# A decode step of two attention and two gated layers: one more quarter of a key cache kept in PSUM, all other products in four banks

## The chip, the cores and the metric

The kernel runs on one core of a Trainium2 chip. The metric is the device time of one execution in microseconds. A difference is given against the kernel before, which computes the same.

## The reference

One token for each of two sequences goes through attention, a gated feed-forward layer, and both again with the same weights and the same caches. All data are fp32.

```python
# B=2, H=32 heads, Sk=8192 cached rows, Dh=128, D=576, Df=4608
def attention(x):                      # x: [B, 1, D], after layernorm
    q = (x @ wq) split into heads
    scores = einsum("bhqd,bhkd->bhqk", q, k_cache) * Dh ** -0.5
    o = einsum("bhqk,bhkd->bhqd", softmax(scores), v_cache)
    return o.reshape(B, 1, H * Dh) @ wo
def glu(x):
    return (gelu(x @ w_gate) * (x @ w_up)) @ w_down
x = x + attention(layernorm(x)); x = x + glu(layernorm(x))
x = x + attention(layernorm(x)); x = x + glu(layernorm(x))
```

A key or value cache of one head of one sequence has 8192 rows of 128 numbers, 4.19 MB. There are 64 of each, so one pass over both caches reads 537 MB, and two passes read them twice, except for what is kept on the chip in between.

## The kernel before

**Items.** Attention works through 64 heads (32 heads, 2 sequences) as 34 items, `ITEMS`: items 0 to 29 are pairs of heads, and the last four, 30 to 33 (`SINGLE[0]` to `SINGLE[3]`), are single heads. The first attention takes the items in rising order, the second in falling order, so that it begins with what the first had last. A pair's keys are 8 parts, a single head's 4 parts; a part is 128 x 2048 fp32, 1.05 MB.

**Space.** One SBUF tile, `space`, holds all that is loaded: six slots of four parts each, the sixth shared with a ring of four places. `Arena` decides at build time which place each load gets and which release it waits for. All loads go through one queue on SyncE, in the order in which `plan_first`, `plan_mlp` and `plan_second` list them. A load is issued when the place that it overwrites is free, and later loads stand behind it.

**Kept items.** At the end of the first attention the keys of items 32 and 33 and the values of items 31, 32 and 33 stay in SBUF (`KEYS_HELD`, `VALUES_HELD`) and are not read again. For kept keys the first attention writes its products elsewhere. The second attention reloads the keys of 31 and 30, first those of 31 into the ring, then those of 30 into the places of the keys of 33 as these are used up, and so on (`plan_second`, `one`).

**One item.** `query` spreads the item's query over the partitions with matmuls (into `qp`, two buffers). For each part, `multiply` forms the products on VectorE (L511), GpSimd adds their halves (L515), and VectorE sums the rest (`add_up`, L518). During the next item's parts the softmax of this item follows: `peak` (maximum, L532, and its transpose `mT`, L534), `highest` (L540, and `nb`, L542), `softmax` (ScalarE, `nbs` at L563 and the exponentials at L565), `total` (`tot`, L574, and its reciprocal, L577 or L582). `values` multiplies the weights with the value cache on TensorE into `acc` (L604). `gather` (L618, L620), `context` (`po`, L629) and `divide` (`oT`, L636 or L645) bring out the head's result, and `project` (L657) adds its part of the output into `xps`.

The order is written out by hand in the loop of `attention`: it is the program's order on every engine, and each engine works in that order. For part 2 of an item it is

```python
if k == 2:
    if p is not None:
        total(p)
    if a is not None:
        gather(a)
        if p < PAIRS:
            context(a)
    if v is not None and v >= 0:
        values(v)
    if a is not None and p >= PAIRS:
        context(a)
```

where `p` is the item before, `v` the item whose values are due, and `a` the one whose accumulator is complete. Where `p` is a single head, the context matmuls stand behind the value matmuls.

**PSUM.** There are eight banks of 128 x 512 fp32. Before, `acc` has two, `xps` one, `po` one, the queries `qp` two, and the other small products (`every4`, `mT`, `nb`, `tot`, with the tag `small`) two. Each is a tile of its own, and waits between engines follow the tiles.

Of the kernel before, what the change touches and what calls it, by code (L numbers as in the profile page):

```python
# [9 lines left out]
F32 = mybir.dt.float32  # L10
# [112 lines left out]
def decode_layers(ctx, tc, x_in, kc, vc, wq, wo, wg, wu, wd, out):  # L123
# [6 lines left out]
    psum1 = ctx.enter_context(tc.tile_pool(name="psum1", bufs=1, space=PSUM))  # L130
    psum2 = ctx.enter_context(tc.tile_pool(name="psum2", bufs=2, space=PSUM))
    ctx.enter_context(tc.manual_schedule())
# [201 lines left out]
    def plan_second():  # L334
# [3 lines left out]
        k63, v63, k62, v62 = ("k", 1, SINGLE[3]), ("v", 1, SINGLE[3]), ("k", 1, SINGLE[2]), ("v", 1, SINGLE[2])  # L338
        for k in range(4):
            one(("k", 1, SINGLE[1]), kc, SINGLE[1], k, None)  # L340
        for k in range(4):
            one(("k", 1, SINGLE[0]), kc, SINGLE[0], k, (k63, k))

        for kind, k in (("k", 0), ("v", 0), ("v", 1), ("k", 1), ("v", 2), ("v", 3), ("k", 2), ("k", 3)):
            if kind == "k":
                one(("k", 1, last), kc, last, k, (k62, k))
            else:
                one(("v", 1, SINGLE[0]), vc, SINGLE[0], k, (v63, k))
        for k in range(4):
            one(("k", 1, last), kc, last, 4 + k, (v62, k))  # L350
        half(("k", 1, last - 1), kc, last - 1, 0, 5)
# [77 lines left out]
    for s in range(2):  # L429
        nc.vector.memset(acc[:, s, :], 0.0)  # L430
    xps = psum1.tile([P, CW], F32, name="xps")
    nc.vector.memset(xps, 0.0)


    def norm(split=False):
# [5 lines left out]
        )  # L441
        every4 = psum2.tile([P, 4 * 6], F32, name="every4", tag="small")
        nc.tensor.matmul(every4, same, apart.rearrange("p c t -> p (c t)"), start=True, stop=True)
# [27 lines left out]
    def attention(layer):  # L471
# [14 lines left out]
        qb, S, prod, rs, mT, rinv, osb = {}, {}, {}, {}, {}, {}, {}  # L486
        po = psum1.tile([P, GH, 2], F32, name="po")

# [3 lines left out]
        def query(n):  # L492

            it = ITEMS[n]
            qb[n] = psum2.tile([P, DH], F32, name="qp")
            for i in range(it.heads):
# [7 lines left out]
        def multiply(n, k):  # L504

            if k == 0:
                S[n] = work.tile([P, SK * 2 // P], F32, name="S")
            u = t = ready[name("k", layer, n)][k]
            if layer == 0 and n in KEYS_HELD:
                u = ready["products"][k % 2]  # L510
# [6 lines left out]
        def add_up(n, k):  # L517
            nc.vector.tensor_reduce(  # L518
                out=S[n][:, k * JC:(k + 1) * JC], in_=prod.pop((n, k)), axis=AX.X, op=ALU.add
            )  # L520
            if layer == 0 and n in KEYS_HELD:
                if n == N - 1 and k >= 2:
                    done(("products", k - 2))
                return
            key = name("k", layer, n)
            done((key, k))
            if k == ITEMS[n].parts - 1:
                ready.pop(key)

        def peak(n):  # L530
            m = work.tile([P, 1], F32, name="m")
            nc.vector.reduce_max(m, S[n][:, :ITEMS[n].rows], axis=AX.X)  # L532
            mT[n] = psum2.tile([1, P], F32, name="mT", tag="small")
            nc.tensor.transpose(mT[n], m, ident)  # L534

        def highest(n):
# [3 lines left out]
            nc.vector.reduce_max(m1[:, :heads], mT.pop(n).rearrange("p (i q) -> p i q", i=heads), axis=AX.X)  # L540
            mT[n] = psum2.tile([P, 2], F32, name="nb", tag="small")
            nc.tensor.matmul(mT[n][:, :heads], ones[0:1, :], m1[:, :heads], start=True, stop=True)  # L542
# [28 lines left out]
        def total(n):  # L571
            it = ITEMS[n]
            tot = psum2.tile([P, 2], F32, name="tot", tag="small")
            nc.tensor.matmul(tot[:, :it.heads], ones, rs.pop(n), start=True, stop=True)  # L574
# [259 lines left out]
```

## Time and profile before

| | us |
|---|---|
| median of 3 runs | 2697.15 |
| lowest and highest run | 2696.98, 2701.9 |
| the profiled execution | 2700.58 |
| its span, first to last instruction | 2698.8 |

The profile is one execution. Its rows give starts in us from the span's start. "PE" is TensorE, "DVE" VectorE, "ACT" ScalarE, "POOL" GpSimd, "SP" SyncE, whose queue issues the loads. A row of the timeline has the start, the duration, the engine, the line of the kernel, what is written and read, the count, and in brackets the idle time of the engine just before with what ended it. A row of the windows has the busy time of each engine in that stretch, the granted TensorE clock, the DMA share and GB/s. Stages: the first attention lasts until about 1295, the first gated layer until about 1373, the second attention until about 2623.

### The profile page before, as it was taken

How to read it: one execution, taken by the hardware profiler on the slowest of the kernel's cores; microseconds unless marked ns; L12 is line 12 of the kernel's file. 1: busy time of each engine (PE TensorE's matmuls, PEld its weight loads, DVE VectorE, ACT ScalarE, POOL GpSimd, SP SyncE). 2: the span in 40 equal slices, each digit the busy share in tenths (PEclk: the TensorE clock that was granted, in tenths of full speed). 3: DMA queues.
4: the chain of work that ended last, by engine and by line, in shares of the span. 5: the costliest groups of instructions: out<-in, count | busy, mean ns of one | idle time of the engine just before them, and what ended most of it. 6: DMA issues, size and time to landing. Idle time of an engine off the chain costs nothing.

```text
span 2698.8 us, 17988 instructions
## 1 busy us (share of the span) xinstructions
PE 900.1 (33%) x7020; PEld 294.0 (11%) x7020; DVE 1872.1 (69%) x1688; ACT 90.0 (3%) x399; POOL 1210.8 (45%) x528
## 2 busy tenths in 40 slices
PE   1323331333233223334644332333233323322355
PEld 0100010001000000111211110001000100000022
DVE  4877787678777776776039887778767867777740
ACT  0000000000000000000000000000000000000000
POOL 2644454445445444544016554445444544544420
PEclk7656656665666566666766665665566566656677
DMA  9999999999999999999999999999999999999998
GB/s 420 435 434 434 434 434 433 433 432 434 435 433 432 435 432 430 433 428 422 403 378 421 429 427 436 435 430 434 434 434 431 434 434 432 434 433 436 432 421 378
DMA packets 33524, 1155.39 MB, mean 428 GB/s; under 512 B 3976, under 2 KB 4000, under 8 KB 5536
## 3 DMA queue, kind: packets, MB, share of 16 engines
q1 hardware_dynamic: 33400, 1154.24, 99.5%
q8 instruction: 55, 0.90, 0.1%
q14 instruction: 29, 0.24, 0.0%
q10 hardware_dynamic: 40, 0.01, 0.0%
HBM read 1154.23 MB, written 0.00 MB: 428 GB/s over the span
## 4 chain that ended last, share of the span: by engine, by line
DMA 82%; DVE 15%; PE 1%; issue 1%; POOL 1%; ACT 0%; SPq 0%; ACTq 0%; DVEq 0%; POOLq 0%
DMA space<-in_A_k_cache_dram 75%; DVE space L511 9%; DVE S L518 5%; DMA space<-in_B_w_up_dram 3%; DMA space<-in_A_wo_dram 2%; DMA space<-in_B_w_down_dram 2%; POOL space L515 1%; DMA space<-in_A_wq_dram 1%; PE acc L742 0%; DMA space<-in_B_w_gate_dram 0%; DMA x<-in_A_x_dram 0%; PE xps L791 0%; PE acc L604 0%; PE acc L478 0%; DVE osb L620 0%
## 5 line engine op out<-in xcount | busy, mean ns | idle before, releaser
L515 POOL TENSOR_TENSOR space<-space 128x1024 f32<-128x1024 f32 x512 | 1206.8, 2357 | 1245.2 <-DVE space L511 1230.4
L511 DVE TENSOR_TENSOR space<-space,qp 128x2048 f32<-128x2048 f32 x512 | 1166.0, 2278 | 591.7 <-DMA space<-in_A_k_cache_dram 567.9
L604 PE MATMUL acc<-space,prz 128*8 128x512 f32 x4096 | 591.3, 740 | 452.2 <-DMA space<-in_A_v_cache_dram 447.6
L518 DVE TENSOR_REDUCE S<-space 128x16 f32<-128x1024 f32 x512 | 618.9, 1209 | 3.4 <-POOL space L515 3.4
L534 PE MATMUL mT<-ident,m 128*1 128x128 f32 x68 | 24.8, 365 | 804.9 <-DVE m L532 804.9
L604 PEld LDWEIGHTS acc<-space,prz 128*8 128x8 f32 x4096 | 118.2, 104 | 868.4 <-DMA space<-in_A_v_cache_dram 452.1
L563 ACT ACTIVATE nbs<-nb 64x1 f32<-64x1 f32 (+1 forms) x128 | 21.2, 166 | 2333.7 <-PE nb L542 2333.0
L534 PEld LDWEIGHTS mT<-ident,m 128*1 128x1 f32 x68 | 5.4, 79 | 821.9 <-issue 786.5
L629 PE MATMUL po<-of,osb 128*32 128x2 f32 x512 | 40.9, 202 | 130.9 <-DVE osb L620 130.9
L542 PE MATMUL nb<-m,unit 1*128 1x2 f32 (+1 forms) x136 | 39.2, 355 | 125.1 <-DVE m L540 125.1
L464 POOL TENSOR_TENSOR rstd<-ve,mhalf 128x1 f32<-128x1 f32 x4 | 2.2, 552 | 170.6 <-DVE ve L462 170.6
L620 DVE SCALAR_TENSOR_TENSOR osb<-acc,diag,osb 128x128 f32<-128x128 f32 x192 | 67.3, 351 | 6.8
L767 DVE STREAM_TRANSPOSE o<-o 128x288 f32<-128x288 f32 x4 | 2.8, 692 | 92.1 <-ACT o L765 92.1
L574 PE MATMUL tot<-sums,unit 128*128 128x2 f32 x120 | 35.2, 363 | 92.1 <-ACT prz L565 92.1
L499 PE MATMUL qp<-qsb,pick 4*64 4x128 f32 (+1 forms) x256 | 30.7, 304 | 80.6 <-DVE space L511 77.3
L468 DVE TENSOR_TENSOR x<-xps,x 128x144 f32<-128x144 f32 x4 | 1.2, 308 | 73.0 <-PE xps L791 42.2
L565 ACT ACTIVATE prz<-S,nbs 64x128 f32<-64x128 f32 (+1 forms) x128 | 50.7, 396 | 12.5 <-POOL prz L555 8.4
L629 PEld LDWEIGHTS po<-of,osb 128*32 128x32 f32 x512 | 35.7, 154 | 139.2 <-DVE osb L620 137.9
L542 PEld LDWEIGHTS nb<-m,unit 1*128 1x128 f32 x136 | 33.3, 303 | 146.3 <-DVE m L540 146.3
L574 PEld LDWEIGHTS tot<-sums,unit 128*128 128x128 f32 x120 | 30.1, 311 | 97.3 <-ACT prz L565 97.3
L791 PE MATMUL xps<-space,hT 128*4 128x144 f32 x576 | 29.8, 374 | 21.0 <-DMA space<-in_B_w_down_dram 19.4
L742 PE MATMUL acc<-space,xt 128*8 128x288 f32 x288 | 30.5, 564 | 18.9 <-DMA space<-in_B_w_up_dram 11.2
(62 smaller groups left out, 294.3 us busy)
## 6 DMA issues: line engine op xcount, KB each, us to landing
space<-in_A_k_cache_dram SPq DMA_DIRECT2D x6, 4096.0 KB
space<-in_A_v_cache_dram SPq DMA_DIRECT2D x6, 4096.0 KB
space<-in_A_wo_dram SPq DMA_DIRECT2D x16, 1152.0 KB
space<-in_A_k_cache_dram SPq DMA_DIRECT2D x16, 1024.0 KB
space<-in_B_w_down_dram SPq DMA_DIRECT2D x9, 1152.0 KB
space<-in_B_w_gate_dram SPq DMA_DIRECT2D x3, 3456.0 KB
space<-in_A_v_cache_dram SPq DMA_DIRECT2D x10, 1024.0 KB
space<-in_A_wq_dram SPq DMA_DIRECT2D x3, 3072.0 KB
```

What stands on the lines that cost most here:

```text
L499: nc.tensor.matmul(qb[n][to, :], pick[32 * c:32 * c + 4, r:r + 1].to_broadcast([4, P // it.heads]), qsb[32 * c:32 * c + 4, (h % 4) * DH:(h ...
L511: nc.vector.tensor_tensor(out=u, in0=t, in1=qb[n].unsqueeze(1).to_broadcast([P, JC, DH]), op=ALU.mult)
L515: nc.gpsimd.tensor_tensor(out=half, in0=half, in1=u[:, :, DH // 2:], op=ALU.add)
L518: nc.vector.tensor_reduce(out=S[n][:, k * JC:(k + 1) * JC], in_=prod.pop((n, k)), axis=AX.X, op=ALU.add)
L534: nc.tensor.transpose(mT[n], m, ident)
L542: nc.tensor.matmul(mT[n][:, :heads], ones[0:1, :], m1[:, :heads], start=True, stop=True)
L565: nc.scalar.activation(pr[at, lo:].rearrange("p (g e) -> p g e", e=4)[:, 0:it.rows // 2:2, :], s[at, :it.rows].rearrange("p (g r) -> p g r ...
L574: nc.tensor.matmul(tot[:, :it.heads], ones, rs.pop(n), start=True, stop=True)
L604: nc.tensor.matmul(accumulator(n)[32 * c:32 * c + 8, :], pr[:, at:at + 8], t[g // 4][:, g % 4 * 4:g % 4 * 4 + 4, :].rearrange("p j d -> p ...
L620: nc.vector.scalar_tensor_tensor(t, q[:, r, :], diag[:, r:r + 1], t, op0=ALU.mult, op1=ALU.add,)
L629: nc.tensor.matmul(po[lo:lo + 32, i, :], t[:, i::GH], of, start=True, stop=True)
L742: nc.tensor.matmul(acc[32 * c:32 * c + 4 * B, h, :HG], window(u, 4 * g + 2 * e), w[:, k, c, :], start=(key == steps[0][0] and k == 0), sto ...
```

## The change

- The queries (two buffers), `xps`, `po` and the other small products (two buffers) move into one PSUM tile `bank` of two banks: queries and `xps` in the first, `po` and the small ones in the second. `acc` keeps its two banks.
- The four banks that are left become a tile `kept` of 128 x 2048. In the first attention ScalarE copies part 3 of the keys of item 31 into it, before the products overwrite that part. In the second attention ScalarE copies it back into the place of item 31's part 0, once that part is summed up.
- `plan_second` loads three parts of item 31 in place of four. All loads behind take a place one earlier: part 0 of item 30 goes into the ring, its parts 1 to 3 and part 0 of item 29 into the places of the keys of 33, and so on. The last place of the values of 32 stays unused.

```diff
-        for k in range(4):
+        for k in range(3):
             one(("k", 1, SINGLE[1]), kc, SINGLE[1], k, None)
         for k in range(4):
-            one(("k", 1, SINGLE[0]), kc, SINGLE[0], k, (k63, k))
-        for kind, k in (("k", 0), ("v", 0), ("v", 1), ("k", 1), ("v", 2), ("v", 3), ("k", 2), ("k", 3)):
+            one(("k", 1, SINGLE[0]), kc, SINGLE[0], k, (k63, k - 1) if k else None)
+        one(("k", 1, last), kc, last, 0, (k63, 3))
+        turns = iter(range(1, 5)), iter(range(4))
+        for kind in "kvvkvvkk":
             if kind == "k":
-                one(("k", 1, last), kc, last, k, (k62, k))
+                k = next(turns[0])
+                one(("k", 1, last), kc, last, k, (k62, k - 1))
             else:
+                k = next(turns[1])
                 one(("v", 1, SINGLE[0]), vc, SINGLE[0], k, (v63, k))
-        for k in range(4):
-            one(("k", 1, last), kc, last, 4 + k, (v62, k))
+        for k in range(5, 8):
+            one(("k", 1, last), kc, last, k, (v62, k - 5))
...
-    xps = psum1.tile([P, CW], F32, name="xps")
+    bank = psum1.tile([P, 2, 512], F32, name="bank")
+    xps = bank[:, 0, 0:CW]
     nc.vector.memset(xps, 0.0)
+    qps = [bank[:, 0, CW + i * DH:CW + (i + 1) * DH] for i in range(2)]
+    po = bank[:, 1, 0:2 * GH].rearrange("p (i c) -> p i c", c=2)
+    smalls = [bank[:, 1, 2 * GH + i * P:2 * GH + (i + 1) * P] for i in range(2)]
+    kept = psum1.tile([P, JC, DH], F32, name="kept")
+
+    def small(p, n):
+        smalls.append(smalls.pop(0))
+        return smalls[0][0:p, 0:n]
...
-            qb[n] = psum2.tile([P, DH], F32, name="qp")
+            qps.append(qps.pop(0))
+            qb[n] = qps[0]
...
             u = t = ready[name("k", layer, n)][k]
+            if n == SINGLE[1] and k == 3 and layer == 0:
+                nc.scalar.copy(kept, t)
...
             key = name("k", layer, n)
+            if layer == 1 and n == SINGLE[1]:
+                if k == 0:
+                    ready[key][3] = ready[key][0]
+                    nc.scalar.copy(ready[key][3], kept)
+                    return
+                k = k % 3
             done((key, k))
...
-            mT[n] = psum2.tile([1, P], F32, name="mT", tag="small")
+            mT[n] = small(1, P)
...
-            mT[n] = psum2.tile([P, 2], F32, name="nb", tag="small")
+            mT[n] = small(P, 2)
...
-            tot = psum2.tile([P, 2], F32, name="tot", tag="small")
+            tot = small(P, 2)
```

More of the change, by code (lines that the diff above doesn't have):

```diff
@@ L130, in decode_layers @@
     psum1 = ctx.enter_context(tc.tile_pool(name="psum1", bufs=1, space=PSUM))
-    psum2 = ctx.enter_context(tc.tile_pool(name="psum2", bufs=2, space=PSUM))
     ctx.enter_context(tc.manual_schedule())
@@ L441, in norm @@
         )
-        every4 = psum2.tile([P, 4 * 6], F32, name="every4", tag="small")
+        every4 = small(P, 4 * 6)
         nc.tensor.matmul(every4, same, apart.rearrange("p c t -> p (c t)"), start=True, stop=True)
@@ L486, in attention @@
         qb, S, prod, rs, mT, rinv, osb = {}, {}, {}, {}, {}, {}, {}
-        po = psum1.tile([P, GH, 2], F32, name="po")
         oT = once.tile([P, H // GH, GH, 2, B], F32, name="oT", tag="part")
@@ L525, in add_up @@
             key = name("k", layer, n)
+            if layer == 1 and n == SINGLE[1]:
[4 more added lines that the diff above has]
+                k = k % 3
             done((key, k))
-            if k == ITEMS[n].parts - 1:
+            if k == ITEMS[n].parts - 1 or not any(c == key for c, _ in arena.live):
                 ready.pop(key)
```

## The prediction

> **What bounds the kernel now.** I read the page first: its span, busy shares, the DMA row and the chain.
>
> ```profile
> span 2698.8 us, 17988 instructions
> PE 900.1 (33%) x7020; PEld 294.0 (11%) x7020; DVE 1872.1 (69%) x1688; ACT 90.0 (3%) x399; POOL 1210.8 (45%) x528
> ...
> DMA  9999999999999999999999999999999999999998
> ...
> DMA 82%; DVE 15%; PE 1%; issue 1%; POOL 1%; ACT 0%; SPq 0%; ACTq 0%; DVEq 0%; POOLq 0%
> ```
>
> The DMA engines are busy nearly throughout, and 82% of the chain is DMA. So a change is worth the bytes it removes plus the idle time that it adds to or takes from the DMA queue, and nothing else. I then read the windows by stage, and the group of the products.
>
> ```profile
> core 0: us, PE busy (x) PEld busy (x) DVE busy (x) ACT busy (x) POOL busy (x), PEclk, DMA share, GB/s
> 1403.00:1404.00 1.00, 0.00 (x0) 0.00 (x0) 1.00 (x1) 0.00 (x0) 1.00 (x1) 0.50 0.20 41
> 1419.00:1468.00 49.00, 25.64 (x149) 7.84 (x141) 46.42 (x42) 1.84 (x9) 30.66 (x13) 0.69 1.01 425
> 1550.00:2540.00 990.00, 297.54 (x2042) 92.07 (x2046) 740.70 (x645) 34.10 (x156) 482.51 (x205) 0.61 1.00 433
> ```
> ```profile
> L511 DVE TENSOR_TENSOR space<-space,qp 128x2048 f32<-128x2048 f32 x512 | 1166.0, 2278 | 591.7 <-DMA space<-in_A_k_cache_dram 567.9
> L484 ACT ACTIVATE qsb<-acc,rstd 128x512 f32<-128x512 f32 x2 | 1.4, 687 | 46.5 <-PE acc L478 46.5
> ```
>
> In the steady stretch (1550 to 2540) the queue runs at 433 GB/s, and VectorE is idle 567.9 us in 57 waits for keys: 10 us of slack in each item. The start of the second attention is the opposite. VectorE is busy 46.42 of 49 us, every load goes into a place that a product or a value matmul must free first, and at 1403 the queue is nearly dry (41 GB/s). There VectorE and TensorE set the time. I therefore read the timeline of that start, engine by engine.
>
> ```profile
> 1413.64 0.28 DVE L540 TENSOR_REDUCE m<-mT 1x1 f32<-1x128 f32 x1 [0.47 <-PE mT L534]
> 1413.85 2.27 DVE L511 TENSOR_TENSOR space<-space,qp 128x2048 f32<-128x2048 f32 x1
> 1414.59 0.17 ACT L563 ACTIVATE nbs<-nb 128x1 f32<-128x1 f32 x1 [18.19 <-PE nb L542]
> 1415.29 0.59 PE L574 MATMUL tot<-rs,unit 128*128 128x1 f32 x2 [0.73 <-ACT prz L565]
> 1415.81 5.13 PE L604 MATMUL acc<-space,prz 128*8 128x512 f32 x32
> 1417.17 2.26 DVE L511 TENSOR_TENSOR space<-space,qp 128x2048 f32<-128x2048 f32 x1
> 1419.37 0.15 DVE L582 RECIPROCAL rinv<-tot 128x1 f32<-128x1 f32 x1
> 1422.88 0.48 PE L499 MATMUL qp<-qsb,pick 4*128 4x128 f32 x2 [1.95 <-DVE space L511]
> 1423.89 2.26 DVE L511 TENSOR_TENSOR space<-space,qp 128x2048 f32<-128x2048 f32 x1
> 1427.32 0.22 DVE L532 TENSOR_REDUCE m<-S 128x1 f32<-128x64 f32 x1
> 1427.45 2.28 DVE L511 TENSOR_TENSOR space<-space,qp 128x2048 f32<-128x2048 f32 x1
> 1427.59 0.37 PE L534 MATMUL mT<-ident,m 128*1 128x128 f32 x1 [4.22 <-DVE m L532]
> 1430.97 2.27 DVE L511 TENSOR_TENSOR space<-space,qp 128x2048 f32<-128x2048 f32 x1
> 1431.80 5.66 PE L604 MATMUL acc<-space,prz 128*8 128x512 f32 x32
> 1437.39 0.43 PE L499 MATMUL qp<-qsb,pick 4*64 4x128 f32 x4
> 1437.69 2.27 DVE L511 TENSOR_TENSOR space<-space,qp 128x2048 f32<-128x2048 f32 x1
> 1448.58 5.80 PE L604 MATMUL acc<-space,prz 128*8 128x512 f32 x32 [2.91 <-DVE osb L620]
> 1449.57 2.28 DVE L511 TENSOR_TENSOR space<-space,qp 128x2048 f32<-128x2048 f32 x1
> 1454.84 0.18 DVE L636 TENSOR_TENSOR oT<-po,rinv 32x16 f32<-32x16 f32 x1 [1.87 <-PE po L629]
> 1455.05 2.29 DVE L511 TENSOR_TENSOR space<-space,qp 128x2048 f32<-128x2048 f32 x1
> 1460.14 0.17 ACT L563 ACTIVATE nbs<-nb 128x1 f32<-128x1 f32 x1 [15.11 <-PE nb L542]
> 1461.35 6.24 PE L604 MATMUL acc<-space,prz 128*8 128x512 f32 x32
> 1462.72 2.26 DVE L511 TENSOR_TENSOR space<-space,qp 128x2048 f32<-128x2048 f32 x1
> 1467.66 0.33 SPq L166 DMA_DIRECT2D space<-in_A_v_cache_dram  x1
> ```
>
> The last row issues the values of item 29. It waits for the end of the value matmuls of item 30 (1461.35 + 6.24 = 1467.59). The window 1419 to 1468 moved 425 GB/s x 49 us = 20.8 MB, and the loads issued for it (12 parts of 1.05 MB, two of 4.19 MB) are 21.0 MB: when this load is issued the queue has under 1 us of work left. Whatever delays that instant delays the rest of the kernel.
>
> **The change part by part.** *Load removed.* One part of 1.05 MB, at 433 GB/s 2.42 us: the whole gain that the change can bring by itself (0.09%).
>
> *Copies added.* Two ScalarE copies of 128x2048. No such row exists; four times the 687 ns of the 128x512 row is 2.75 us, the upper end; for below, a copy hidden entirely, zero. I take nothing: the one in the second attention sits between the sum of item 31's part 0 and the product of part 3, and a product with its sum (1427.45 to 1430.97, 3.5 us) lies between. ScalarE is 3% busy. Uncovered it would cost at most 2.75 us.
>
> *Waits added.* Every small product now lies in one PSUM tile, `bank`. The list of the built instructions with their waits shows what that does: of 512 products, 249 wait for TensorE (4 before) and 68 for ScalarE (none before); the matmuls of `tot` wait for VectorE (none did). Three of its rows, around items 33 and 32:
>
> ```
> L529 TensorTensor space<-space,bank 128x2048 [waits Activation_49]
> L599 Matmult bank<-rs,unit 128x1 [waits DVE_49,Activation_49]
> L515 Matmult bank<-qsb,pick 128x128 [waits DVE_49]
> ```
>
> (L529 is the product, L599 `tot`, L515 the query.) Engines take turns on the whole tile. That such turns can be by tile and not by address is in the old trace: the matmuls at 1448.58 write one bank of `acc` and waited 2.91 us for VectorE, which read the other.
>
> In the program's order the new waits are these. An item's first product waits for the next item's query, which TensorE runs behind the value matmuls. The second waits for the transposed maximum (in items 32 and 29 for ScalarE's `nbs` too). `tot` waits for the third product to end, and the reciprocal for `tot`; the value matmuls are queued behind `tot`. Item 30's fourth product waits for the context matmuls, behind the value matmuls. Step by step, with rows above (delay against before in brackets):
>
> - Item 32, second product: `nbs` ends 1414.76, so it starts 1414.83 [1.0]. The third ends at 1417.17 + 2.26 + 1.0 = 1420.4; then `tot` 0.59 and the reciprocal at 1421.1 against 1419.37 [1.7]. Value matmuls follow `tot` by 0.52: 1421.0 + 5.13 = 1426.1, then the query, 0.48.
> - Item 31, first product 1426.7 against 1423.89 [2.8]. Second: `m` ends 0.09 after the old start, the transpose takes 0.05 + 0.37: [3.4]. Third ends 1430.97 + 2.27 + 3.4 = 1436.6; values 1437.2 + 5.66 = 1442.9; query 0.43.
> - Item 30, first product 1443.4 against 1437.69 [5.7]; transpose [6.2]; `tot` [6.9]; so the value matmuls start at 1455.5 and the context is done where the old oT step began, 1454.84 + 6.9 = 1461.7. The fourth product starts there, not at 1449.57 [12.2]. Its sum, oT and the query follow (2.2 + 1.2 + 0.2 + 0.5).
> - Item 29, first product 1465.9 against 1455.05 [10.8]; second waits for `nbs` (old end 1460.31): [11.8]; third ends 1462.72 + 2.26 + 11.8 = 1476.8; values 1477.3 + 6.24 = 1483.6. The values of 29 are issued at 1483.6, not 1467.66: **16.0 us later**.
>
> By then the queue is empty, so the 2.42 us saved are part of that idle time and not a gain on top. Afterwards nothing adds: the next issues wait for products 12 us late, while their predecessors land 16 late. I take 16, the value by the rows of this very stretch. The ends: 7.6 if all four groups of value matmuls run as fast as the quickest row of the trace (below), and 21 if each takes 6.24 (2.1 more in all) and the copy is uncovered (2.75). Below zero it cannot go, since the queue is dry at that issue already.
>
> *First attention's tail.* The same waits act there.
>
> ```profile
> 1223.46 2.28 DVE L511 TENSOR_TENSOR space<-space,qp 128x2048 f32<-128x2048 f32 x1
> 1231.65 2.29 DVE L511 TENSOR_TENSOR space<-space,qp 128x2048 f32<-128x2048 f32 x1 [2.17 <-issue]
> 1260.86 3.62 PE L604 MATMUL acc<-space,prz 128*8 128x512 f32 x32 [0.23 <-DMA space<-in_A_v_cache_dram]
> 1276.29 1.04 PE L604 MATMUL acc<-space,prz 128*8 128x512 f32 x8 [1.44 <-DMA space<-in_A_v_cache_dram]
> 1281.58 2.06 SPq L281 DMA_DIRECT2D space<-in_A_wo_dram  x2
> 1281.84 1.40 PE L657 MATMUL xps<-space,oT 128*4 128x144 f32 x32 [0.30 <-DMA space<-in_A_wo_dram]
> ```
>
> Item 31's last product (1223.46) moves behind the context matmuls and item 32 starts near 1234.4, not 1231.65 [2.75]; a transpose (0.54) and a `tot` (0.6) each in items 32 and 33 make it near 5. The value matmuls of 33 waited for their last piece until 1276.29; started near 1276.6 they take 3.6 (the 1260.86 row) and end 1280.2, not 1277.33 [2.9]; with the projection's new wait for oT the output weights of 1281.58 are issued 3.3 later. Behind the weights that arrived at 1281.84 two more transfers of 1.18 MB are queued, 2.8 us each at 425 GB/s, so the last arrives at 1287.4, 5.8 us after the old issue. I estimate 2 us between an issue to an empty queue and the first bytes (the dip of the 1403 window is of that length) and as much between the last bytes and the release. So 3.3 + 2 - (5.8 - 2) = 1.5 us of idle, between 0 and 4; I take 1.6.
>
> *Steady items.* Transpose, second `nbs` and `tot` add 1.8 us to VectorE in each; the 10 us of idle hide it.
>
> Sum: 16 + 1.6 = 17.6 us. On the profiled execution (2700.58, span 2698.8) that gives 2718.2; the median of the runs is 3.4 lower, so 2697.15 + 17.6 = **2714.8 us**.
>
> **The rivals.**
> - *The waits hide, and only the load counts.* Then 2697.15 - 2.4 = 2694.7, not slower. For it: 82% of the chain is DMA. It decides if engines take turns only where they share a bank: the products read the query's bank, while maxima, `tot` and context lie in the other. Then only the queries cost, 0.2 to 0.5 us, and no query ends late, so 2694.7 to 2697.7. Against: the built list has the waits on the whole tile. The Trainium skill (PSUM — Partial Sum Buffer, "PSUM bank collisions raise a hardware error") says that two engines must be kept apart by bank and group of 32 partitions, reads against reads included; by that rule this rival's price holds, and the trace's wait at 1448.58, across banks, goes further than the rule. Chance 0.08.
> - *TensorE runs faster there.* With 3.62 us for each of the four groups of value matmuls instead of 5.13, 5.66, 5.80 and 6.24 the delay falls by 8.4: 2697.15 + 7.6 + 1.6 = 2706.4. Against: these groups start after pauses, now longer ones. Chance 0.14.
> - *The steady items don't hide it.* 1.8 us in each of 56 items is 101: 2816. Against: 10 us of idle. Chance 0.05.
> - That the load isn't gone can be set aside: the built list has one transfer fewer.
>
> **How the numbers follow.** The forecast has the other 0.73. Two tenths of a per cent, 5.4 us, is about what a measurement of this kernel can tell from no change. Of the first rival's 0.08, 0.06 lie within it, and 0.02 are for faster by more, which needs a gain larger than the load. All other cases are slower: 0.92. The range runs from just under the faster TensorE (2705) to the upper ends of both terms (21 + 4: 2722).
>
> **What would show it.** The changed profile should have the products waiting for TensorE in long pieces (3, 6, 12 us late at items 31, 30 and at item 30's fourth product), the values of 29 issued some 16 us later relative to the first product of item 33, the DMA share falling between 1440 and 1500, 1154.3 MB in place of 1155.39, and steady items 38.7 us apart as before. A DMA share as full there as before, or steady items further apart, would prove me wrong.

## The result and the profile after

| | before | changed |
|---|---|---|
| median of 5 runs each, us | 2697.64 | 2720.37 |
| lowest to highest | 2696.98 to 2702.33 | 2719.31 to 2721.55 |
| profiled execution (span) | 2700.58 (2698.8) | 2719.31 (2717.4) |

The ratio is 1.0076, with a 95% interval of 1.0065 to 1.0088: slower by 0.65 to 0.88%, 17.5 to 23.7 us. The five runs of before lay low: in the next comparison 27 runs of the same kernel have a median of 2700.4 (2697.27 to 2703.46). Against that the change costs 20.0 us; between the two profiled executions it is 18.7 us.

The page of the changed kernel:

```profile
span 2717.4 us, 17981 instructions
PE 895.8 (33%) x7020; PEld 293.3 (11%) x7020; DVE 1889.7 (70%) x1688; ACT 93.6 (3%) x401; POOL 1209.6 (45%) x528
...
DMA  9999999999999999999987999999999999999998
DMA packets 33380, 1154.34 MB, mean 425 GB/s; under 512 B 3960, under 2 KB 3984, under 8 KB 5520
```

One load fewer has gone through (1154.34 MB against 1155.39), VectorE has the same 1688 instructions, and the DMA is no longer full in slices 21 and 22. The windows say where (columns as in the prediction's windows; the first row is the stretch that held 46.42 us of VectorE and 425 GB/s before):

```profile
1419.00:1468.00 49.00, 20.91 (x126) 6.71 (x126) 38.47 (x35) 2.97 (x7) 25.44 (x11) 0.71 0.86 350
1468.00:1500.00 32.00, 8.54 (x41) 2.43 (x41) 29.88 (x21) 0.61 (x3) 19.50 (x10) 0.55 0.68 285
1550.00:2540.00 990.00, 299.64 (x2085) 91.47 (x2077) 742.87 (x634) 32.83 (x150) 480.73 (x205) 0.62 1.00 433
```

The steady stretch is as full as before, 433 GB/s. The start of the second attention is not. The DMA view of the changed kernel from 1400 to 1510, in 40 slices of 2.75 us, shows the hole itself:

```profile
DMA  9358979193999999998579899991000988888999
GB/s 420 155 179 295 346 325 363 39 357 77 399 414 426 429 429 426 414 423 363 164 298 512 381 369 381 429 489 48 0 0 0 381 381 381 381 381 381 477 620 429
```

In the slice from 1474 to 1477 the queue moves 48 GB/s, and in the three behind it, to 1485, nothing. It waits until a place for the values of item 29 comes free. The timeline of the changed kernel shows why that place is late (DVE is VectorE; L529 is the product, L599 `tot`, L629 the value matmuls, L654 the context):

```profile
1399.65 4.48 DVE L529 TENSOR_TENSOR space<-space,bank 128x2048 f32<-128x2048 f32 x2 [22.50 <-PE bank L515]
1423.71 5.26 PE L629 MATMUL acc<-space,prz 128*8 128x512 f32 x32
1429.42 2.29 DVE L529 TENSOR_TENSOR space<-space,bank 128x2048 f32<-128x2048 f32 x1 [0.99 <-PE bank L515]
1437.15 1.84 ACT L548 COPY space<-kept 128x2048 f32<-128x2048 f32 x1
1439.39 0.56 PE L599 MATMUL bank<-rs,unit 128*128 128x1 f32 x2 [2.83 <-DVE space L529]
1439.88 5.70 PE L629 MATMUL acc<-space,prz 128*8 128x512 f32 x32
1441.19 2.28 DVE L529 TENSOR_TENSOR space<-space,bank 128x2048 f32<-128x2048 f32 x1
1445.99 2.29 DVE L529 TENSOR_TENSOR space<-space,bank 128x2048 f32<-128x2048 f32 x1 [1.40 <-PE bank L515]
1458.19 5.08 PE L629 MATMUL acc<-space,prz 128*8 128x512 f32 x32 [1.67 <-DVE osb L645]
1463.73 2.29 DVE L529 TENSOR_TENSOR space<-space,bank 128x2048 f32<-128x2048 f32 x1 [4.47 <-PE bank L654]
1467.88 2.29 DVE L529 TENSOR_TENSOR space<-space,bank 128x2048 f32<-128x2048 f32 x1 [0.54 <-PE bank L515]
1473.17 2.29 DVE L529 TENSOR_TENSOR space<-space,bank 128x2048 f32<-128x2048 f32 x1 [0.88 <-ACT nbs L588]
1479.42 6.41 PE L629 MATMUL acc<-space,prz 128*8 128x512 f32 x32
1485.89 0.33 SPq L165 DMA_DIRECT2D space<-in_A_v_cache_dram  x1
```

Read down the brackets. Products wait for queries (0.99, 1.40, 0.54), for the context (4.47) and for ScalarE (0.88), and `tot` waits for a product (2.83); in the rows of before it waited for ScalarE (0.73). Each wait passes its delay to the next through the value matmuls.

**A yardstick for the start of the second attention.** Two rows mark it in every kernel: the first product of all, and the first product of item 25, which waits for its keys in a full queue. Before and after:

```profile
1396.98 4.48 DVE L511 TENSOR_TENSOR space<-space,qp 128x2048 f32<-128x2048 f32 x2 [20.64 <-PE qp L499]
1587.35 2.29 DVE L511 TENSOR_TENSOR space<-space,qp 128x2048 f32<-128x2048 f32 x1 [9.70 <-DMA space<-in_A_k_cache_dram]
```
```profile
1606.06 2.29 DVE L529 TENSOR_TENSOR space<-space,bank 128x2048 f32<-128x2048 f32 x1 [7.78 <-DMA space<-in_A_k_cache_dram]
1644.76 2.29 DVE L529 TENSOR_TENSOR space<-space,bank 128x2048 f32<-128x2048 f32 x1 [7.62 <-DMA space<-in_A_k_cache_dram]
```

Before it is 1587.35 - 1396.98 = 190.4 us, after 1606.06 - 1399.65 = 206.4: 16.0 us more. A second profile of before gives 189.9, so half a microsecond between two profiles can be chance. I call this the **start length**. It does not contain what came earlier: the first product itself is 2.67 us later (1399.65 against 1396.98), and 16.0 + 2.7 = 18.7 us is the whole difference of the two profiles.

### The profile page after: what moved, and what is told of

The parts are those of the page before. It is cut to its first block, busy times and chain, and to the rows that moved or that the text cites. A ratio compares the mean times of both kernels' runs of the same rounds, so it can differ in the third digit from the quotient of the medians.

```text
span 2717.4 us, 17981 instructions
## 1 busy us (share of the span) xinstructions
PE 895.8 (33%) x7020; PEld 293.3 (11%) x7020; DVE 1889.7 (70%) x1688; ACT 93.6 (3%) x401; POOL 1209.6 (45%) x528
## 2 busy tenths in 40 slices
DMA packets 33380, 1154.34 MB, mean 425 GB/s; under 512 B 3960, under 2 KB 3984, under 8 KB 5520
## 4 chain that ended last, share of the span: by engine, by line
DMA 81%; DVE 14%; PE 3%; issue 1%; POOL 0%; ACT 0%; SPq 0%; DVEq 0%; ACTq 0%; POOLq 0%
DMA space<-in_A_k_cache_dram 72%; DVE space L529 9%; DVE S L536 4%; DMA space<-in_B_w_up_dram 3%; DMA space<-in_A_v_cache_dram 2%; DMA space<-in_B_w_down_dram 2%; PE acc L629 1%; DMA space<-in_A_wo_dram 1%; DMA space<-in_A_wq_dram 1%; POOL space L533 0%; PE bank L682 0%; DMA x<-in_A_x_dram 0%; PE acc L767 0%; PE bank L816 0%; DVE osb L645 0%
## 5 line engine op out<-in xcount | busy, mean ns | idle before, releaser
L529 DVE TENSOR_TENSOR space<-space,bank 128x2048 f32<-128x2048 f32 x512 | 1168.6, 2283 | 558.2 <-DMA space<-in_A_k_cache_dram 459.8
L629 PE MATMUL acc<-space,prz 128*8 128x512 f32 x4096 | 591.1, 741 | 334.1 <-DMA space<-in_A_v_cache_dram 330.7
L559 PE MATMUL bank<-ident,m 128*1 128x128 f32 x68 | 25.0, 368 | 728.0 <-DVE m L557 728.0
L629 PEld LDWEIGHTS acc<-space,prz 128*8 128x8 f32 x4096 | 118.3, 104 | 749.9 <-issue 415.2
L588 ACT ACTIVATE nbs<-bank 64x1 f32<-64x1 f32 (+1 forms) x128 | 21.2, 166 | 2357.1 <-PE bank L567 2356.4
L599 PE MATMUL bank<-sums,unit 128*128 128x2 f32 x120 | 33.5, 349 | 203.8 <-DVE space L529 202.3
L567 PE MATMUL bank<-m,unit 1*128 1x2 f32 (+1 forms) x136 | 39.4, 356 | 165.8 <-DVE m L565 165.8
L515 PE MATMUL bank<-qsb,pick 4*64 4x128 f32 (+1 forms) x256 | 31.8, 311 | 156.9 <-DVE space L529 146.3
L654 PE MATMUL bank<-of,osb 128*32 128x2 f32 x512 | 40.9, 202 | 103.5 <-DVE osb L645 103.5
L567 PEld LDWEIGHTS bank<-m,unit 1*128 1x128 f32 x136 | 33.5, 304 | 185.5 <-DVE m L565 185.5
L599 PEld LDWEIGHTS bank<-sums,unit 128*128 128x128 f32 x120 | 30.1, 312 | 207.3 <-issue 205.7
L654 PEld LDWEIGHTS bank<-of,osb 128*32 128x32 f32 x512 | 35.7, 154 | 111.7 <-DVE osb L645 110.5
L602 DVE RECIPROCAL rinv<-bank 128x2 f32<-128x2 f32 x60 | 10.2, 171 | 46.5 <-PE bank L599 46.5
```

The lines of the kernel that those rows point to most:

```text
L515: nc.tensor.matmul(qb[n][to, :], pick[32 * c:32 * c + 4, r:r + 1].to_broadcast([4, P // it.heads]), qsb[32 * c:32 * c + 4, (h % 4) * DH:(h ...
L529: nc.vector.tensor_tensor(out=u, in0=t, in1=qb[n].unsqueeze(1).to_broadcast([P, JC, DH]), op=ALU.mult)
L588: nc.scalar.mul(nbs[at], nb[at, i:i + 1], -scale)
L629: nc.tensor.matmul(accumulator(n)[32 * c:32 * c + 8, :], pr[:, at:at + 8], t[g // 4][:, g % 4 * 4:g % 4 * 4 + 4, :].rearrange("p j d -> p ...
L654: nc.tensor.matmul(po[lo:lo + 32, i, :], t[:, i::GH], of, start=True, stop=True)
```

## The experiments

**1. Only the shared tile.** The kernel before with the tile `bank`, without the kept part, its copies and the changed order of loads.

```diff
-    xps = psum1.tile([P, CW], F32, name="xps")
+    bank = psum1.tile([P, 2, 512], F32, name="bank")
+    xps, qps, po, smalls = ...        # as in the change
...
-            tot = psum2.tile([P, 2], F32, name="tot", tag="small")
+            tot = small(P, 2)
```

> The kernel before, with the one PSUM tile for queries, xps, po and small products, and nothing else of the change: four loads of item 31, no kept part, no copies. Theory (turns by whole tile set the time; the removed load fell into an idle stretch of the queue): the values of item 29 are issued as late as in the changed kernel, 15.6 us later against the first product of item 33 than before, the queue is idle for about 7.5 us there in place of 9.9, and the time is that of the changed kernel, about 2720 us (2718.5 to 2722). Rival, the removed load is a gain of 2.4 us on top of the waits: 2722.8. Rival, the copies and the kept part cost the time: under 2716.

Measured: 2719.64 us, ratio 1.0073 (1.0061 to 1.0086) against 27 runs of before on the same chip; 1.0076 (1.0065 to 1.0088) was that of the change. Its values of item 29 are issued here:

```profile
1397.61 4.49 DVE L522 TENSOR_TENSOR space<-space,bank 128x2048 f32<-128x2048 f32 x2 [21.55 <-PE bank L510]
1484.96 0.33 SPq L165 DMA_DIRECT2D space<-in_A_v_cache_dram  x1
```

That is 87.35 us behind its first product; in the changed kernel it is 86.24, before 70.68 (16.7 later than before, 15.6 expected). So the whole loss comes with the shared tile, and the load that the change removes buys nothing that these runs can see. A gain of 2.4 us on top of the waits would have given 2722.8, above every one of the five runs (2717.67 to 2721.29); but the two ratios come from two comparisons, and their intervals of some 3 us to either side alone would not exclude it. The start length is 207.3, 0.9 more than in the changed kernel. That need be no sign of the load either: the four groups of value matmuls took 23.34 us in sum here and 22.45 there.

**2. Two tiles in place of one.** The changed kernel, the shared tile cut at the bank.

```diff
-    bank = psum1.tile([P, 2, 512], F32, name="bank")
-    xps = bank[:, 0, 0:CW]
+    front = psum1.tile([P, 512], F32, name="front")    # xps, queries
+    back = psum1.tile([P, 512], F32, name="back")      # po, small products
+    xps = front[:, 0:CW]
...
```

> The changed kernel, with the one tile cut into two tiles of one bank each (queries and xps; po and the small products). Theory: products wait only for the next item's query, and the query finds TensorE free since totals no longer wait for products. In the old trace that makes item 30's first product 0.2 us later and item 29's 0.5 us, and the first product of all waits for both queries, 0.5 us. The load's 2.4 us stay worthless since the values of 29 are issued to a dry queue: 2697.6 + 1.2 = 2698.8 us (2697 to 2700.5). Rival, the load counts: 2696.4. Rival, something else than the tile (the copies, the moved places) made the changed kernel slow: over 2710.

Measured: 2701.95 us (11 runs), ratio 1.0006 (0.9997 to 1.0015). The time that was expected, 2697 to 2700.5, was reckoned from the low median of 2697.6 and is missed; the expected difference, 1.2 us, lies in the interval, and the kernel is not told apart from before. The slowness is gone with the kept part, the copies and the moved places all in place. Its timeline:

```profile
1432.98 1.85 ACT L549 COPY space<-kept 128x2048 f32<-128x2048 f32 x1
1436.20 2.27 DVE L530 TENSOR_TENSOR space<-space,front 128x2048 f32<-128x2048 f32 x1
1440.46 2.29 DVE L530 TENSOR_TENSOR space<-space,front 128x2048 f32<-128x2048 f32 x1 [0.86 <-PE front L516]
1452.36 2.28 DVE L530 TENSOR_TENSOR space<-space,front 128x2048 f32<-128x2048 f32 x1
1458.28 2.29 DVE L530 TENSOR_TENSOR space<-space,front 128x2048 f32<-128x2048 f32 x1 [0.19 <-PE front L516]
```

Two query waits are left, 0.86 and 0.19; item 30's fourth product (1452.36) waits for no context. The start length is 192.0.

**3. Without the copies.**

```diff
-            if n == SINGLE[1] and k == 3 and layer == 0:
-                nc.scalar.copy(kept, t)
...
-                    nc.scalar.copy(ready[key][3], kept)
```

> As the kernel with two tiles, but neither copy is made: part 3 of item 31 in the second attention is multiplied from what lies in the place of part 0, so the output is not the reference's. Theory: both copies are covered (in the changed profile the second one takes 1.84 us and ends 2.2 us before its product), so the time is that of the two-tile kernel within 0.7 us. Rival, a copy stands on the path: 1.8 us less, or 3.7 us for both.

Measured: 2700.76 us, ratio 1.0002 (0.9993 to 1.0011). By times this is undecided: 1.2 us below the two-tile kernel, with intervals that overlap. The start length is 189.7, 2.3 us shorter, but the rows above show that the copy ends at 1434.83 and its product starts at 1436.20 without a wait. What differs first between the two profiles is the pace of the value matmuls of item 32, which take nothing from the copy (two-tile kernel first):

```profile
1433.64 6.40 PE L630 MATMUL acc<-space,prz 128*8 128x512 f32 x32
```
```profile
1433.02 4.89 PE L626 MATMUL acc<-space,prz 128*8 128x512 f32 x32
```

The slower group makes the next query late (the 0.86 us above). Whether the copy, which runs beside this group, is what slows it is the question of experiment 12.

**4. The kernel before again.**

> The kernel before once more, for a second profile. Its runs so far lie at 2697.0 to 2697.6 and at 2701.9 to 2702.3, and its first profile at 2700.6. Theory: a profile at the lower level shows one idle stretch of the DMA queue less, of 3 to 5 us, near one of the places where the queue is nearly dry (1303 to 1310, 1378 to 1383, 1403 to 1422, 1468). Rival: the levels differ by the rate of the DMA throughout, and no single place shows it.

Measured: 2699.11 us (2697.76 to 2700.96). Both theories fall with the 27 runs: there are no two levels, the times fill 2697 to 2703 without a gap between two groups. The second profile reaches its first product 1.29 us earlier (1395.69) and its start length is 0.5 us shorter. The values of item 32 take 5.00 us in it, 5.66 in the first profile. The spans differ by 2.0 us, so no single stretch makes the whole difference.

**5. The context ahead of the value matmuls.** In the changed kernel, one tile kept.

```diff
-                        if p < PAIRS:
-                            context(a)
+                        context(a)
                     if v is not None and v >= 0:
                         values(v)
-                    if a is not None and p >= PAIRS:
-                        context(a)
```

> The changed kernel, but where the item before is a single head the context matmuls stand ahead of the value matmuls, as for pairs. In the changed profile the fourth product of item 30 starts at 1463.73, 4.47 us after it could, because the context stands behind the values. Theory (a product waits for what is behind it in the one tile): it starts right after the sum, near 1459.3; the values start 0.6 us later, so the first product of item 29 is 3.5 us earlier and the values of item 29 are issued 3.5 us earlier; the first attention's item 31 gains its 5.4 us wait in the same way, of which at most 1.5 us reach the end. 5 us less than the changed kernel, 2715.4 us (2714 to 2717.5). Rival, the one tile's cost lies in the totals and queries alone and the wait for the context is covered: within 1 us of the changed kernel, 2719.5 to 2721.5.

Measured: 2711.93 us, ratio 1.0040 (1.0027 to 1.0053): 8.4 us below the changed kernel, more than the 5 expected and below the expected 2714 to 2717.5. From its timeline:

```profile
1396.25 4.49 DVE L529 TENSOR_TENSOR space<-space,bank 128x2048 f32<-128x2048 f32 x2 [21.29 <-PE bank L515]
1456.77 2.28 DVE L529 TENSOR_TENSOR space<-space,bank 128x2048 f32<-128x2048 f32 x1
1478.15 0.33 SPq L165 DMA_DIRECT2D space<-in_A_v_cache_dram  x1
```

The fourth product (1456.77) waits for nothing now. The start length is 202.0, 4.4 less than in the changed kernel, near the 3.5. The rest is ahead of it: the first product comes 3.4 us earlier. Of that the edit explains the part that the context cost at the first attention's end, where the queue moved 418 GB/s from 1200 to 1300 as before, against 402 in the changed kernel; chance may be up to 3 us (see the first attention's tail, below).

**6. Queries and totals in one tile, all else apart.** On the kernel before.

```diff
+    front = psum1.tile([P, 512], F32, name="front")
+    qps = [front[:, i * DH:(i + 1) * DH] for i in range(2)]
+    tots = [front[:, 2 * DH + 2 * i:2 * DH + 2 * i + 2] for i in range(2)]
...
-            tot = psum2.tile([P, 2], F32, name="tot", tag="small")
+            tots.append(tots.pop(0))
+            tot = tots[0]
```

> The kernel before, with only the queries and the totals in one tile of one bank; everything else as before (all loads, no copies). Theory: totals wait for the third product and the value matmuls stand behind the totals, so the next query, and with it the next first product, is late: by the rows of before 2.3 us at item 31, 4.6 at item 30, 5.8 at item 29, and the values of item 29 are issued 9.9 us late, 0.5 more from the wait of the very first product: 10.4 us over the kernel before, 2711 us where that runs at 2700.4 (2708.5 to 2713). Rival, transposes and context carry the cost and the totals are covered: within 2 us of the kernel before.

Measured: 2709.57 us, 8.5 above the 2701.05 of before on that chip; ratio 1.0030 (1.0019 to 1.0042). The start length is 199.1, 8.8 more than before (9.9 expected). So about half of the 16 us comes from queries and totals alone, with no transpose and no context in the tile:

```profile
1420.62 0.56 PE L579 MATMUL front<-rs,unit 128*128 128x1 f32 x2 [5.03 <-DVE space L515]
1426.75 2.29 DVE L515 TENSOR_TENSOR space<-space,front 128x2048 f32<-128x2048 f32 x1 [0.93 <-PE front L503]
1443.07 2.29 DVE L515 TENSOR_TENSOR space<-space,front 128x2048 f32<-128x2048 f32 x1 [1.59 <-PE front L503]
```

`tot` waits 5.03 us for a product, and from there the first products of items 31 and 30 wait for their queries (0.93 and 1.59), that of item 29 for 0.19.

**7. Two tiles, and the next query made after an item's first product.**

```diff
-            if not last:
-                query(seq[i + 1])
...
                 multiply(n, k)
+                if k == 0 and not last:
+                    query(seq[i + 1])
```

> The kernel with two tiles, but each next query is made after the first product of the item instead of ahead of it, so that no first product waits for it. Theory: nothing is late any more, and the removed load is worth nothing since the values of 29 are still issued by the chain of VectorE and TensorE to a queue that has run dry: the time of the kernel before on the same chip within 1 us, and about 1.3 us below the two-tile kernel. Rival, the load counts as soon as no wait stands against it: 2.4 us below the kernel before.

Measured: 2700.92 us, ratio 0.9998 (0.9989 to 1.0007): the kernel before. Behind the first product of all only the second waits for a query in the start (0.88 us), 1.05 MB are gone, and the time stays. A gain of 2.4 us (0.9991) is not excluded by the interval; the start length, 191.8 against 190.4 and 189.9, does not show one.

**8. Halves, in the changed kernel.** The values of 29, the keys of 27 and the values of 28 are loaded in two halves each.

```diff
-        cache(("v", 1, last), vc, last)
+        for src, kind, n, at in ((vc, "v", last, 0), (kc, "k", last - 2, 2), (vc, "v", last - 1, 0)):
+            half((kind, 1, n), src, n, 0, at)
+            half((kind, 1, n), src, n, 4, at + 1)
...
```

> The changed kernel, but the values of item 29, the keys of item 27 and the values of item 28 in the second attention are loaded as two halves of 4.19 MB, each issued when its own half of the place is free. Theory: the 9.9 us of idle queue before the values of 29 stand behind the place of the values of item 30, and the other half of the place is free near 1476.7, after the sum of item 29's part 0; so the idle stretch of 12.2 us shrinks to about 3, and some 2.5 us are lost again at the values of 28, whose place is released late: 6.5 us less than the changed kernel, 2714 us (2711 to 2716). Rival, VectorE is behind by 16 us and stays the limit whatever the queue does: within 1.5 us of the changed kernel.

Measured: 2712.15 us, ratio 1.0042 (1.0029 to 1.0055), 8.2 below the changed kernel, within the expected range; between the two profiled executions it is 4.8. Its DMA view over the same 110 us, and the issue of the two halves of the values of 29:

```profile
DMA  9859989283999999999199899995688997999998
1477.79 9.65 SPq L165 DMA_DIRECT2D space<-in_A_v_cache_dram  x2
```

The hole of four slices is down to two half-filled ones. The first product of all comes at 1399.63, as in the changed kernel (1399.65), and the first half is issued at 1477.79, where the changed kernel issued the whole load at 1485.89. The start length is 201.4: 5.0 of the 16.0 are back with nothing done about the waits, and the rival falls. So this part was lost because loads of 8.39 MB ask for two places at once and wait for the later; three were split together, and their shares were not run apart. The other 11 us are untouched by it.

**9. Halves, in the kernel before.** The same edit.

> The kernel before, with the values of item 29, the keys of 27 and the values of 28 in the second attention loaded as two halves. Theory: in the old trace the queue loses 1.4 us before the values of 29; with its first half issued early this idle time goes and nothing else changes: 1.4 us less than the kernel before on the same chip (0 to 2.5 less). Rival, the queue is full there and the gap is only the pace of the DMA: no change.

Measured: 2699.98 us, ratio 0.9999 (0.9991 to 1.0008); start length 189.4. The expected 1.4 us is inside the interval and so is zero: inconclusive.

**10. and 11. Two tiles, later queries and halves; and then the keys of item 28 in pieces.** The eleventh adds to the tenth:

```diff
-        half(("k", 1, last - 1), kc, last - 1, 0, 5)
-        half(("k", 1, last - 1), kc, last - 1, 4, 4)
+        for k in (1, 2, 0, 3):
+            quarter(("k", 1, last - 1), kc, last - 1, k, 5 * SLOT + k * PART)
+        for k in range(4):
+            quarter(("k", 1, last - 1), kc, last - 1, 4 + k, 4 * SLOT + k * PART)
```

(`quarter` loads one part into a given place when that place is free.)

> The kernel with two tiles and later queries, with the same three loads in halves. Theory: with the queue kept full at the values of 29 the removed load becomes worth its 2.4 us, on top of the 1.4 us of the halves: 3.8 us less than the kernel before (2.5 to 5 less), and 2.4 less than the kernel before with halves. Rival, the kept quarter is worth nothing in any order, since later loads are still released by VectorE: the same as the kernel before with halves.

> As the kernel with two tiles, later queries and halves, and the keys of item 28 are loaded in eight pieces of 1.05 MB, each when its own place is free (parts 1 and 2 ahead of part 0). In the profile of the kernel with halves the queue still idles about 1.7 us before the two halves of these keys, because the last ring place now holds part 0 of item 30 and comes free one product later than item 31's part 3 did. Theory: this idle time goes as well, so that the removed load is worth its 2.4 us: 3.8 us less than the kernel before on the same chip (2 to 5 less), and in its profile the idle time of the queue from the first release to the values of 28 is about that of the kernel before with halves, 8.5 us. Rival, the gain ends in other idle time further on, since VectorE releases each later place when it did before: no more than 1 us less than the kernel before.

Measured: 2699.55 us, ratio 0.9997 (0.9988 to 1.0006), and 2698.72 us, ratio 0.9995 (0.9986 to 1.0004). Neither is told apart from before. The marks of the eleventh:

```profile
1398.52 2.29 DVE L546 TENSOR_TENSOR space<-space,front 128x2048 f32<-128x2048 f32 x1 [21.57 <-PE front L532]
1586.53 2.29 DVE L546 TENSOR_TENSOR space<-space,front 128x2048 f32<-128x2048 f32 x1 [9.69 <-DMA space<-in_A_k_cache_dram]
```

The start lengths run 191.8 (experiment 7), 188.7 (halves), 188.0 (pieces), against 190.4 and 189.9 before and 189.4 before with halves (in the first three the second product waits 0.88 us for a query, which lies within the length). With halves the length is 0.7 us shorter than that of before with halves, where 2.4 was expected, and the times of these two differ by 0.4 (2699.55 and 2699.98). The pieces bring another 0.7, but they were not tried in the kernel before, so that it isn't known whether the removed load has a part in it. Set against half a microsecond of chance, the profiles hint at a part of the load's 2.4 us and don't show it. From 1430 to 1530 the queue moved 429 GB/s with halves, 432 with pieces and 435 in before with halves. In the time the gain of the eleventh is at most 3.8 us, and zero is not excluded. No kernel here beats the one before beyond doubt.

**12. The last kernel without the copies.** The edit is that of experiment 3.

> As the kernel with two tiles, later queries, halves and pieces, but without both copies (part 3 of item 31 in the second attention is multiplied from what lies in the place of part 0). In four profiles with the copy beside the value matmuls of item 32 these take 6.08 to 6.40 us and the granted clock falls from the first group of value matmuls to that one; in four of kernels without it they take 4.89 to 5.66 and the clock rises in three of them. Theory: the copy slows TensorE there, so that without it the group takes about 5.0 us, the clock rises, and the start length falls by 1 to 2.5 us from 188.0. Rival: the clock has its own course and the copy nothing to do with it: a group anywhere from 4.9 to 6.4 us, a start length of 187.5 to 188.5, since each group hides behind the products there.

Measured: 2697.85 us, ratio 0.9996 (0.9987 to 1.0005); start length 187.6. The value matmuls of item 32, with the copies and without:

```profile
1433.96 6.19 PE L646 MATMUL acc<-space,prz 128*8 128x512 f32 x32
```
```profile
1431.51 6.19 PE L642 MATMUL acc<-space,prz 128*8 128x512 f32 x32
```

And the windows of the kernel without them (granted clock third from the end), over the groups of items 33, 32 and 31:

```profile
1416.00:1424.00 8.00, 5.17 (x32) 0.81 (x24) 8.00 (x7) 0.00 (x0) 6.02 (x3) 0.77 0.81 325
1430.00:1440.00 10.00, 7.25 (x40) 1.90 (x39) 10.00 (x8) 0.61 (x3) 6.80 (x4) 0.66 1.01 421
1447.00:1456.00 9.00, 6.75 (x40) 1.69 (x40) 6.46 (x9) 0.00 (x0) 4.53 (x2) 0.62 1.01 422
```

The clock falls without a copy as well (0.77, 0.66, 0.62), and the group is as long to 0.01 us, 6.19. So the theory falls in all its numbers: a slow group there doesn't need the copy, and the start length fell by 0.4 us and not by 1 to 2.5. This is one profile. The four with the copy beside this group had 6.08 to 6.40 us, and of the five without the copy and without a shared tile only this one is above 5.66, so that some effect of the copy on the group is not excluded; on the time none is seen.

## Why the prediction came out

The forecast was 2714.8, 17.6 us over before; measured were 22.7 over the first five runs of before, 20.0 over the median of 27, and 18.7 between the profiles. The mechanism and its size in the second attention were right; the term of the first attention's tail came out near its size in part by luck (below).

**The chain, step by step** (each row's delay against before, less the 2.67 us by which all started later):

| step | forecast | measured |
|---|---|---|
| first product of item 31 (1429.42) | 2.8 | 2.9 |
| first product of item 30 (1445.99) | 5.7 | 5.6 |
| its fourth product (1463.73) | 12.2 | 11.5 |
| first product of item 29 (1467.88) | 10.8 | 10.2 |
| value matmuls of item 30 start (1479.42) | 15.95 | 15.4 |
| values of 29 issued (1485.89) | 16.0 | 15.6 |
| start length | 16 | 16.0 |

Experiment 6 splits it: 8.8 us by queries and totals. Experiment 5 takes back 4.4 by the context. The transposes' share was not run by itself. The second rival, a faster TensorE, fell: the four groups of value matmuls took 5.26, 5.70, 5.08 and 6.41 us, 22.45 in sum against 22.83 before.

**First attention's tail.** This term was sized too small, by about a microsecond if the profiles are taken as they are. The step that failed is the estimate that the values of 33 start near 1276.6 and end at 1280.2. The changed profile:

```profile
1278.03 4.74 PE L629 MATMUL acc<-space,prz 128*8 128x512 f32 x32
1286.54 1.31 SPq L280 DMA_DIRECT2D space<-in_A_wo_dram  x2
```

They start 1.4 later and end 2.6 later than forecast, since the piece-wise start with the data (1270.64 before) had become one block behind the projection. So the output weights were issued 5.0 us late, not 3.3, and the first product of the second attention came 2.7 us late, not 1.6 (with the wait for both queries in it). But that instant varies: in the eleven profiles without this tail (experiment 5's, with its context ahead, is one of them) it lies between 1395.51 and 1398.82. The three with it have 1399.65, 1397.61 and 1399.63, on average 1.8 above the mean of those eleven.

What the prediction lacks here is that part of the loss comes back. The windows over the tail and over the gated layer behind it, changed kernel first, then before:

```profile
1200.00:1300.00 100.00, 45.80 (x489) 19.66 (x479) 52.11 (x63) 4.21 (x13) 31.13 (x17) 0.69 0.96 402
1300.00:1400.00 100.00, 61.58 (x654) 18.88 (x654) 7.36 (x28) 2.63 (x7) 1.10 (x2) 0.69 1.01 414
1200.00:1300.00 100.00, 45.78 (x482) 19.69 (x486) 51.22 (x63) 2.45 (x12) 29.38 (x17) 0.67 0.99 418
1300.00:1400.00 100.00, 60.21 (x646) 18.37 (x638) 9.12 (x24) 2.62 (x7) 1.21 (x2) 0.69 0.99 403
```

At 433 GB/s the tail lost 3.7 us of transfer (402 against 418 over 100 us), and the next 100 us won 2.5 of them back (414 against 403; before, the queue was not full there). About a microsecond of that is chance: from 1300 to 1392 the second profile of before moved 406 GB/s, the first 401. So the 1.6 us fit what is left, 1.2, partly by luck. Of the estimate's two terms of 2 us, the first, from an issue to the first bytes, is not the same everywhere: behind 1286.54 the queue moved 129 GB/s from 1287 to 1288 and 424 only from 1289 on, but behind 1485.89 it moved 590 from 1486 to 1487. The second, from the last bytes to the release, no run shows.

**The removed load.** "Part of that idle time and not a gain on top": experiments 1 and 7 agree. The lower end of the first rival's price, 2694.7 to 2697.7, did not follow this: it took the load as a gain of 2.4 us although the values of 29 would still be issued to a dry queue. In experiment 2 the time was 2701.95 against 2700.4 for before, and 2.4 less lies outside the interval. By the prediction's own reading that rival should have stood at its upper end, no gain and 0.5 us for the queries.

**The copies.** Taken as nothing. They took 1.84 and 1.86 us, under the bound of 2.75, and the second ends 2.2 us ahead of its product (1437.15 + 1.84 against 1441.19). Experiment 12 finds the start length 0.4 us shorter without them, which is within the half microsecond between two profiles of one kernel.

**Steady items.** 1644.76 - 1606.06 = 38.7 us an item, as was expected. The cost that was forecast as hidden, 1.8 us in 56 items or 101 us, is there as lost slack: VectorE's wait for keys falls from 567.9 to 459.8 us, by 108 (the row of the waits, after: us in total, times, longest).

```profile
DVE space L529 <- DMA space<-in_A_k_cache_dram: 459.8, 57, 23.9
```

**Turns by bank.** The first rival's condition, engines that take turns only within a bank, was made true in experiment 2, and with it nearly all of the loss went (ratio at most 1.0015, 4 us). The Trainium skill (PSUM — Partial Sum Buffer, "PSUM bank collisions raise a hardware error") asks that engines be kept apart by bank and group of 32 partitions, and lets them work on different banks at the same time. The run agrees: in experiment 2 TensorE wrote `tot` into one bank from 1433.13 on, while a product read the query in the other (1432.82 to 1435.09). The waits across the two banks came with the one tile.

**The median.** The forecast moved the profiled 2718.2 down by 3.4 to the median of three runs. That median was of a low sample; without the step the forecast is 1.1 us from the changed kernel's profiled 2719.31. The forecast's whole miss, 5.6 us to the median of 2720.37, is these 3.4, these 1.1, and the 1.1 between the profiled execution and that median.

## What to carry to other kernels

Waits follow tiles: putting products of several engines into one tile to save room makes each take turns with all others, and where two engines already alternate on the path (here at the start of a stage, not in its steady part) those turns add up; a tile per bank took nearly all of the loss away. Ask of a removed byte whether the queue is full where it goes: look for the next issue that is bound by a release, and expect the saving to end there if the queue is dry, as 2.4 us did here within what these runs can tell. A load that asks for two places at once waits for the later one, and splitting three such loads gave back 5 of 16 us without touching the cause.

## What the runs showed of the hardware

The same 32 value matmuls at the same point of the kernel took 4.89 to 6.40 us from profile to profile (experiment 3), with a granted clock of 0.53 to 0.83 over the window from 1430 to 1440; in two profiles of the kernel before alone it was 5.66 and 5.00. I had priced them by one profile's rows. And one kernel, unchanged, spreads over 6 us (2697.27 to 2703.46 in 27 runs), so that a median of five can be 2.8 us off the median of 27, more than the load in question.
